# Second rows' DMA transpose placed inside the sequence of loads, with a new load sequence and instruction order

## The chip, the cores and the metric

The kernel runs on one core of a Trainium2 chip. The metric is the device time of one execution in microseconds (us). TensorE (PE in the profile) does matrix products and transposes into PSUM, VectorE (DVE) and ScalarE (ACT) do elementwise work and copy PSUM out, GpSimd (POOL) does small helpers, and SyncE (SP) issues nearly all transfers; ACT's queue issues the rest.

## The reference

Rows of `A_q` (2048 x 512, bf16) are normalized to `xn`. Two branches use them: a gated MLP with 1792 hidden columns, and a short shifted product of `k` and `v` followed by a long causal convolution with a filter as long as the sequence, written with FFTs. The result is `x + s * silu(mlp)`.

```
def reference(A_q, A_k, A_v, A_shift_k, A_ssm_k, A_ssm_D, B_x, B_w_gate, B_w_up, B_w_down):
    def _A_ref(q, k, v, shift_k, ssm_k, ssm_D):
        ks = shift_k.shape[-1]                                  # 4 taps
        k_pad = jnp.pad(k, ((0, 0), (ks - 1, 0), (0, 0)))
        for t in range(ks):
            k_shift = k_shift + k_pad[:, t:t + S, :] * shift_k[:, ks - 1 - t][None, None, :]
        kv = k_shift * v
...
        y = irfft(rfft(kv) * rfft(ssm_k))[:S] + kv * ssm_D
        return q * y
    def _B_ref(x, w_gate, w_up, w_down):
        h = _gelu(x @ w_gate) * (x @ w_up)
        return h @ w_down
    x = A_q
    xn = _layernorm(x, axis=-1)
    s = _A_ref(xn, A_k, A_v, A_shift_k, A_ssm_k, A_ssm_D)
    g = _silu(_B_ref(xn, B_w_gate, B_w_up, B_w_down))
    return x + s * g
```

(The FFT lines are condensed.)

## The kernel before

**Rows.** The 2048 rows lie as 16 tiles of 128, in four groups q = 0 to 3 (first to fourth rows). `ln(q)` normalizes a group: `bn_stats` and `bn_aggr` on DVE, a power on POOL, then `XN`. `xn_transpose(q)` makes `xnT`, the layout that the products need: for q = 0 by PE transposes of `XN`, copied out by ACT and DVE; for q > 0 by one DMA transpose on SP. `xnT` has two buffers, so the third rows take the first rows' one.

**MLP.** `unit(q, m)` is one of 14 column blocks: four matmuls with `Wg`, four with `Wu` (128x512 each; for q = 0 and m < 2 in halves of 256 columns), GELU on ACT into `GE`, and the product `HT` on DVE. `down(q)` multiplies `HT` by `Wd`, 14 matmuls for each row tile.

**Convolution.** It is a two-stage transform written as matmuls. The filter `Hn` (four loads) is transposed by PE into `HTr` (`h_transpose`, 16 transposes a load) and multiplied by the first-stage matrix in `TB` (rows `psall<-HTr,TB`), copied by ACT to `ASH` and stored to the DRAM scratch `ZH`. `kshift(i)` computes the shifted product for a group of rows on DVE into `V` (`KAC`, `KTM` and `V`, eight steps of 128x2048), which needs the loads of `KK`, `V` and the taps `SKR`, spread by POOL to `SKB`. `V` goes through the same stage (rows `psall<-V,TB`) to `ZK`. Second stages read back `BH` and `BK` in 32-row tiles; the filter's spectrum goes to `ZS` and comes back as `HS`. `spectrum(n)` for n = 0 to 7 multiplies (`HB`, `KS` on DVE) and transforms back with `TT`, the DMA transpose of `TB`; results go through `ZI`, come back as `BI`, and a last matmul with `TT` gives y.

**What sets the order.** Nothing is ordered by hand. `Sched.add` records a task with its engine, its estimated duration, what it reads and writes, and a priority; `Sched.run` walks through estimated time, always taking the engine that can start first and on it the task with the lowest priority number among those that could start within `SLACK`. The result fixes the instruction order on each engine; `Trk` adds the semaphore waits. The `P_` numbers are priorities. Loads are tasks of a pseudo-engine `loads`, in the order of the string `ORDER`: a = a single tile of the first rows (odd ones on ACT's queue), h = a quarter of the filter, w = a chunk of `Wg` and `Wu`, k and v = a quarter of `KK` and `V`, x = a later group of rows, d = half of `Wd`, s = `Drow`, `SKR` and the three small pieces of `KK`. All loads are issued ahead of everything else on SP; the DMA transposes, stores and scratch loads come behind the last of them. `hold` puts `N_HOLD` matmuls on zeros between the two halves of the first rows' transposes.

The lines on which the change bears most:

```
order = S.run()
order.sort(key=lambda t: 0 if t is t_zero else 1 if t.eng == "loads" else 2)
for t in order:
    t.emit(t.eng)
```

Of the kernel before, what the change touches and what calls it, by code (L numbers as in the profile page):

```python
# [14 lines left out]
DM = 512  # L15
# [9 lines left out]
ORDER = "a0 a1 h0 a2 a3 w0 h1 w1 h2 w2 h3 s0 w3 k0 v0 w4 x1 k1 v1 d0 d1 k2 v2 k3 v3 x2 x3"  # L25
# [13 lines left out]
P_KB = 30.904
P_PI = -42.641  # L40
P_LN1 = -49.977
P_LN2 = 65.105
P_LN3 = 20.555
N_HOLD = 3
P_H1 = -92.083
P_K1 = 58.537
P_KSH = 8.63
P_KV = -83.839
P_BH = -76.098
P_H2 = -49.07  # L50
P_H2E = 103.626
P_K2 = -54.197
P_MUL = 9.87
P_BO = -5.789
P_ZI = -56.979
P_Q0 = 100.795
P_DN = 126.799
P_GE = -54.936
P_HT = -22.28
P_TA = 11.975  # L60
P_TG = -10.089
P_BI = -97.551
P_Y = -98.812
P_YD = -118.206
P_GX = 100.186
P_OD = -78.816
P_CW = -46.946
P_WS = -85.41
P_SW = -56.976
P_HTR = 9.192  # L70
P_SKB = 105.503
P_SG = 65.13
P_SU = 9.136
# [394 lines left out]
def build_kernel(nc, A_q, A_k, A_v, A_shift_k, A_ssm_k, A_ssm_D, B_w_gate, B_w_up, B_w_down, out):  # L468
    with ExitStack() as es0:
# [414 lines left out]
        def xn_transpose(q):  # L884
            af = gu_tasks[q - 2] if q >= 2 else (skb if q else [])
# [397 lines left out]
```

## Time and profile before

| what | value |
|---|---|
| median of 3 runs | 210.4 us (208.4, 210.4, 211.3) |
| profiled execution | 209.09 us, of which the span is 207.3 us |
| granted TensorE clock, mean | 0.992 |
| DMA traffic | 57.06 MB, mean 275 GB/s |
| ACT copies after the filter's first stage | 16 of 1.0 us |
| store of a filter tile to `ZH`, issue to landing | 6.8 us median |

The profile shows one execution. Its span runs from the first to the last recorded work; the run's own time is 1.8 us longer. "Busy" is the time an engine executes; a wait is put down to whatever came last before the engine went on. The row of busy tenths cuts the span into 40 slices, and DMA traffic by slice shows the loads of the first quarter:

```profile
DMA  6999999999923289999989999997997413397953
GB/s 182 320 365 332 359 394 394 398 418 361 251 68 152 100 274 287 321 307 369 310 272 292 243 304 352 401 353 269 356 298 273 159 54 104 121 343 223 310 219 103
```

One slice is 5.2 us. The DMA engines are full in the first ten slices and nearly idle in the twelfth.

### The profile page before, as it was taken

What the parts mean: (1) busy time and instruction counts of PE and PEld (TensorE: products, weight loads), DVE (VectorE), ACT (ScalarE), POOL (GpSimd) and SP (SyncE); (2) the same over time, 40 slices, a digit from 0 to 9 for tenths busy, and PEclk for the clock granted to TensorE, in tenths of its full rate; (3) what the DMA queues carried; (4) which work ended last, traced back from release to release, by engine and by line L of the source; (5) the groups of instructions that cost most, each with busy time, mean ns of one, the idle gap of its engine ahead of it and who ended that gap; (6) DMA issues with size and microseconds to landing.
All of it is one profiled execution on the core that took longest, in us unless ns stands there. A gap on an engine that the chain in (4) does not pass through costs nothing.

```text
span 207.3 us, 3599 instructions
## 1 busy us (share of the span) xinstructions
PE 191.6 (92%) x1404; PEld 86.3 (42%) x1404; DVE 150.2 (72%) x245; ACT 130.3 (63%) x168; POOL 10.1 (5%) x21
## 2 busy tenths in 40 slices
PE   7699999996199999999998898999999999999993
PEld 2485444442044444343343333334344334444452
DVE  7788289989429989998894384676776672338994
ACT  6245776786066878988966486777787694441111
POOL 2201301003000000000120000000000000000000
PEclk9999999999889999999999999999999999999999
DMA  6999999999923289999989999997997413397953
GB/s 182 320 365 332 359 394 394 398 418 361 251 68 152 100 274 287 321 307 369 310 272 292 243 304 352 401 353 269 356 298 273 159 54 104 121 343 223 310 219 103
DMA packets 43623, 57.06 MB, mean 275 GB/s; under 512 B 11091, under 2 KB 31447, under 8 KB 42582
## 3 DMA queue, kind: packets, MB, share of 16 engines
q1 hardware_dynamic: 36662, 48.18, 70.3%
q10 hardware_dynamic: 6944, 8.65, 12.2%
q8 instruction: 11, 0.18, 0.3%
q14 instruction: 6, 0.05, 0.1%
HBM read 35.78 MB, written 18.87 MB: 264 GB/s over the span
## 4 chain that ended last, share of the span: by engine, by line
PE 65%; DMA 25%; DVE 5%; issue 2%; ACT 2%; SPq 1%; DVEq 0%
PE psall L674 60%; DMA xnT<-XN 13%; DMA HS<-ZS 5%; DMA KK<-in_A_k_dram 5%; PE psall L1022 4%; DMA X<-in_A_q_dram 2%; SPq L650 1%; DVE KS L1087 1%; DVE HB L1087 1%; DVE HT L1129 1%; DVE KTM L1003 1%; ACT xnT L670 1%; PE psall L898 1%; ACT AST L670 0%; PE psall L928 0%
## 5 line engine op out<-in xcount | busy, mean ns | idle before, releaser
L674 PE MATMUL psall<-xnT,Wg 128*128 128x512 bf16 (+1 forms) x232 | 55.3, 376 | 7.5 <-DMA xnT<-XN 6.7
L1129 DVE TENSOR_TENSOR HT<-psall,GE 128x512 bf16<-128x512 f32 x56 | 38.3, 689 | 26.3 <-PE psall L674 23.6
L674 PE MATMUL psall<-xnT,Wu 128*128 128x512 bf16 (+1 forms) x232 | 55.4, 373 | 0.0
L674 PE MATMUL psall<-Wd,HT 128*128 128x512 bf16 (+1 forms) x238 | 51.5, 367 | 0.0
L1126 ACT ACTIVATE GE<-psall 128x512 bf16<-128x512 f32 x56 | 32.3, 600 | 22.9 <-PE psall L674 22.9
L674 PEld LDWEIGHTS psall<-xnT,Wg 128*128 128x128 bf16 x232 | 22.1, 98 | 34.7 <-issue 8.1
L674 PEld LDWEIGHTS psall<-Wd,HT 128*128 128x128 bf16 x238 | 22.9, 98 | 25.7 <-issue 1.3
L674 PEld LDWEIGHTS psall<-xnT,Wu 128*128 128x128 bf16 x232 | 21.6, 98 | 26.6 <-issue 3.7
L670 ACT ACTIVATE BO<-psall 128x1024 bf16<-128x1024 f32 x16 | 16.4, 1025 | 7.1 <-DMA ZI<-BO 3.1
L1155 DVE SCALAR_TENSOR_TENSOR G<-G,psall 128x512 bf16<-128x512 bf16 x12 | 8.2, 687 | 14.6 <-ACT G L1153 14.5
L670 ACT ACTIVATE ASH<-psall 128x1024 bf16<-128x1024 f32 x16 | 15.9, 1023 | 3.9 <-PE psall L674 3.9
L670 ACT ACTIVATE KB<-psall 128x1024 bf16<-128x1024 f32 x16 | 16.0, 1026 | 1.8 <-PE psall L1022 1.4
L1005 DVE TENSOR_TENSOR KAC<-KAC,KTM 128x2048 bf16<-128x2048 bf16 x12 | 15.1, 1262 | 0.2
L1087 DVE TENSOR_TENSOR HB<-KB,HS 128x1024 bf16<-128x1024 bf16 x16 | 11.0, 686 | 5.8 <-DMA HS<-ZS 5.2
L1003 DVE TENSOR_TENSOR KTM<-KK,SKB 128x2048 bf16<-128x2048 bf16 x12 | 14.6, 1217 | 0.1
L1040 ACT ACTIVATE AST<-psall 128x1024 bf16<-128x1024 f32 x11 | 11.1, 1027 | 4.7 <-DMA ZS<-AST 3.0
L863 DVE BATCH_NORM_STATS2 stats<-X 128x6 f32<-128x512 bf16 x16 | 10.5, 675 | 2.0 <-DMA X<-in_A_q_dram 2.0
L1161 ACT ACTIVATE G<-psall 128x512 bf16<-128x512 f32 (+1 forms) x5 | 2.6, 512 | 15.0 <-PE psall L674 15.0
L1087 DVE TENSOR_TENSOR KS<-KB,HS 128x1024 bf16<-128x1024 bf16 x16 | 11.0, 685 | 0.0
L670 ACT ACTIVATE AST<-psall 128x1024 bf16<-128x1024 f32 x9 | 9.2, 1025 | 2.4 <-PE psall L674 2.4
L1153 ACT ACTIVATE G<-psall 128x512 bf16<-128x512 f32 x12 | 7.1, 608 | 5.7 <-PE psall L674 5.5
L674 PE MATMUL psall<-HTr,TB 128*128 128x512 bf16 x32 | 9.5, 395 | 0.4 <-DVE HT L1129 0.4
(73 smaller groups left out, 149.0 us busy)
## 6 DMA issues: line engine op xcount, KB each, us to landing
HS<-ZS SPq DMA_DIRECT2D x16, 512.0 KB, 6.0
ZH<-ASH ACTq DMA_DIRECT2D x16, 256.0 KB, 6.8
BH<-ZH SPq DMA_DIRECT2D x8, 512.0 KB, 5.1
BK<-ZK SPq DMA_DIRECT2D x8, 512.0 KB, 6.1
ZI<-BO ACTq DMA_DIRECT2D x16, 256.0 KB, 3.9
BI<-ZI SPq DMA_DIRECT2D x16, 256.0 KB, 4.4
ZS<-AST SPq DMA_DIRECT2D x11, 256.0 KB, 4.3
ZK<-AST SPq DMA_DIRECT2D x9, 256.0 KB, 3.8
```

Of the source, the lines that this page charges most:

```text
L670: return h.activation(o, i, ACTF.Copy)
L674: return h.matmul(o, lhsT=l, rhs=r, start=st, stop=sp)
L863: t_stats[t] = op([("DVE", 670.0)], lambda e, h, t=t: h.bn_stats(stats[:, t, :], X[:, t, :]), r=[bX[q][t % 4]], w=[bst[t]], rr=[R_X[t]], w ...
L1003: op([("DVE", dur)], lambda e, h, j=j, m=m: h.tensor_tensor(KTM[:, m.slot, :, :], kk(j), sk(j), ALU.mult), r=need + [bSKB[j], a], w=[m], r ...
L1005: op([("DVE", dur)], lambda e, h, m=m: h.tensor_tensor(KAC[:, a.slot, :, :], KAC[:, a.slot, :, :], KTM[:, m.slot, :, :], ALU.add), r=[m], ...
L1022: trk.op("PE", lambda h: h.matmul(ps(s, i)[b, :], lhsT=w(col)[a, :], rhs=data(col)[a, :], start=n < 16, stop=n >= len(todo) - 16, tile_pos ...
L1040: op([("ACT", act(1024))], lambda e, hd, p=p, a=a: hd.activation(ast["K"][a.slot].rearrange("p c d -> p (c d)"), ps(psl(p)), ACTF.Copy, sc ...
L1087: op([("DVE", dve(1024, 2))], lambda e, hd, h=h, k=k, o=o, T=T: hd.tensor_tensor(flat(T, o), flat(KB, kb[h]), flat(HS, hs, (k, 2 * h)), AL ...
L1126: op([("ACT", act(512))], lambda e, h: h.activation(GE[:, g.slot, :], bank(pg), ACTF.Gelu_apprx_tanh), r=[pg], w=[g], rr=lambda: R_bank(pg ...
L1129: op([("DVE", dve(512, 1))], lambda e, h: h.tensor_tensor(HT[:, q % 2, m, :], bank(pu), GE[:, g.slot, :], ALU.mult), r=[pu, g], w=[bHT[q][m]],
L1153: op([("ACT", act(n))], lambda e, h, g=g, pc=pc: h.activation(g, pc(), ACTF.Tanh, scale=0.5), r=[p], w=[bt], rr=lambda p=p: R_bank(p), ww= ...
L1155: op([("DVE", dve(512, 1))], lambda e, h, g=g, pc=pc: h.scalar_tensor_tensor(out=g, in0=g, scalar=1.0, in1=pc(), op0=ALU.add, op1=ALU.mult ...
```

## The change

- The string `ORDER` is new. The four filter loads come right behind the first rows' tiles; weights follow from chunk 4 to chunk 0; and a new entry `t1` puts the second rows' DMA transpose between the loads k2 and v2, so that v2, v1 and x2 are issued behind it on SP.
- For that, `xn_transpose(1)` adds its task to `loads` with the duration `T_XT`, and no longer waits for the tap copies `skb`. The emission loop issues the loads ahead of `t1` first, and from `t1` on those behind it at the place where `t1` stands in the order.
- `hold` and `N_HOLD` go: three matmuls on zeros.
- The transpose of `TB` no longer waits for the last load by name; it follows it on SP anyway.
- The estimate of load times is by a rate for each load instead of by bytes loaded so far, and loads are taken strictly in sequence. `SLACK`, `HEDGE`, `QUEUE`, `DEFER` and all 39 `P_` numbers are new. These set the order alone.

No other instruction is added or removed.

```
-ORDER = "a0 a1 h0 a2 a3 w0 h1 w1 h2 w2 h3 s0 w3 k0 v0 w4 x1 k1 v1 d0 d1 k2 v2 k3 v3 x2 x3"
+ORDER = "a0 a1 h3 a3 h2 a2 h0 h1 k0 w4 w3 x1 s0 w1 v3 k1 w2 w0 x3 d0 k3 d1 v0 k2 t1 v2 v1 x2"
...
+T_XT = 2400.0
...
-P_XT = -23.014
-P_G1 = -95.843
+P_XT = -67.6853007
+P_G1 = -45.5396678
...
-N_HOLD = 3
...
-    SLACK = 90.163
+    SLACK = 96.23327505813286
...
-    QUEUE = {"ACT": 1017.717, "DVE": 26555.1}
+    QUEUE = {"ACT": 1232.4012520764104, "DVE": 429041.2336871297}
...
-    DEFER = 8815.075
+    DEFER = 6968771.228794256
...
-        def hold(e):
-            for i in range(N_HOLD):
...
+        xt_at = {}
         for what in ORDER.split():
             i = int(what[1:])
+            if what[0] == "t":
+                n_load[0] += 1
+                xt_at[i] = n_load[0]
+                continue
...
-            af = gu_tasks[q - 2] if q >= 2 else (skb if q else [])
+            af = gu_tasks[q - 2] if q >= 2 else []
...
-                S.add([("SP", 4400.0)], f, r=bXN[4 * q:4 * q + 4], w=bxnT[q], prio=-1 if q < 3 else P_XT, nbytes=1.6 * 524288, after=af)
+                if q in xt_at:
+                    S.add([("loads", T_XT)], lambda e: f("SP"), r=bXN[4 * q:4 * q + 4], w=bxnT[q], prio=xt_at[q], lat=1500.0)
+                else:
+                    S.add([("SP", 4400.0)], f, r=bXN[4 * q:4 * q + 4], w=bxnT[q], prio=-1 if q < 3 else P_XT, nbytes=1.6 * 524288, after=af)
...
-        g1_tasks = [S.add([("SP", 4400.0)], tt, r=[bF, bTW, bTS], w=[bTT], prio=P_G1, nbytes=1.6 * 589824, after=last_load)]
+        g1_tasks = [S.add([("SP", 4400.0)], tt, r=[bF, bTW, bTS], w=[bTT], prio=P_G1, nbytes=1.6 * 589824)]
...
-        order.sort(key=lambda t: 0 if t is t_zero else 1 if t.eng == "loads" else 2)
+        loads = [t for t in order if t.eng == "loads"]
+        turn = next(i for i, t in enumerate(loads) if not t.nbytes)
+        for t in [t_zero, *loads[:turn]]:
+            t.emit(t.eng)
         for t in order:
-            t.emit(t.eng)
+            for x in loads[turn:] if t is loads[turn] else [t] if t.eng != "loads" and t is not t_zero else []:
+                x.emit(x.eng)
```

**Place 1: the second rows' transpose.** SP's queue from the last loads to the first stores, before:

```order
L650 DMA Wd<-in_B_w_down_dram 128x7x512 x2
L650 DMA KK<-in_A_k_dram 128x2048
L650 DMA V<-in_A_v_dram 128x2048
L650 DMA KK<-in_A_k_dram 128x2048
L650 DMA V<-in_A_v_dram 128x2048
L650 DMA X<-in_A_q_dram 128x2048 x2
L889 DMA_TRANSPOSE xnT<-XN 128x16x128
L1057 DMA_TRANSPOSE TT<-TB 128x18x128
L650 DMA ZK<-AST 128x1024 x3
L650 DMA ZK<-ASX 128x1024
```

and now:

```order
L659 DMA KK<-in_A_k_dram 128x2048
L659 DMA Wd<-in_B_w_down_dram 128x7x512
L659 DMA V<-in_A_v_dram 128x2048
L659 DMA KK<-in_A_k_dram 128x2048
L898 DMA_TRANSPOSE xnT<-XN 128x16x128
L659 DMA V<-in_A_v_dram 128x2048 x2
L659 DMA X<-in_A_q_dram 128x2048
L1066 DMA_TRANSPOSE TT<-TB 128x18x128
L659 DMA ZK<-AST 128x1024 x3
L659 DMA ZK<-ASX 128x1024
```

The transpose `xnT<-XN` moved from behind the last load to ahead of the last three (v2, v1, x2). PE's queue at the end of the first rows and the start of the second rows (the first `Wg` row behind `Wd` is the second rows' first gate matmul), before:

```order
L674 MATMUL psall<-HTr,TB 128x512 x4
L674 MATMUL psall<-xnT,Wu 128x256 x4
L674 MATMUL psall<-HTr,TB 128x512 x4
L674 MATMUL psall<-Wd,HT 128x512 x28
L674 MATMUL psall<-xnT,Wg 128x512 x4
L674 MATMUL psall<-HTr,TB 128x512 x2
L674 MATMUL psall<-xnT,Wu 128x512 x4
```

and now:

```order
L683 MATMUL psall<-Wd,HT 128x512 x4
L683 MATMUL psall<-HTr,TB 128x512 x2
L683 MATMUL psall<-Wd,HT 128x512 x23
L683 MATMUL psall<-V,TB 128x512 x4
L683 MATMUL psall<-Wd,HT 128x512 x5
L683 MATMUL psall<-V,TB 128x512 x2
L683 MATMUL psall<-Wd,HT 128x512 x5
L683 MATMUL psall<-V,TB 128x512 x2
L683 MATMUL psall<-Wd,HT 128x512 x5
L683 MATMUL psall<-xnT,Wg 128x512 x8
```

42 matmuls with `Wd` and 8 with `V` now stand ahead of the second rows, 28 and none before; the last four with `HTr` moved ahead of them too.

**Place 2: the start.** PE's queue behind the warm-up matmuls, before:

```order
L928 MATMUL psall<-ident,Hn 128x128 x16
L898 MATMUL psall<-ident,XN 128x128 x8
L674 MATMUL psall<-AST 128x512 x3
L674 MATMUL psall<-xnT,Wg 128x256 x4
L674 MATMUL psall<-xnT,Wu 128x256 x4
L928 MATMUL psall<-ident,Hn 128x128 x16
L898 MATMUL psall<-ident,XN 128x128 x8
L674 MATMUL psall<-xnT,Wg 128x256 x4
L674 MATMUL psall<-xnT,Wu 128x256 x4
L928 MATMUL psall<-ident,Hn 128x128 x16
L674 MATMUL psall<-xnT,Wg 128x256 x4
L674 MATMUL psall<-xnT,Wu 128x256 x4
```

and now:

```order
L937 MATMUL psall<-ident,Hn 128x128 x32
L910 MATMUL psall<-ident,XN 128x128 x8
L937 MATMUL psall<-ident,Hn 128x128 x32
L910 MATMUL psall<-ident,XN 128x128 x8
L683 MATMUL psall<-HTr,TB 128x512 x4
L683 MATMUL psall<-xnT,Wg 128x512 x8
L683 MATMUL psall<-xnT,Wu 128x512 x4
L683 MATMUL psall<-HTr,TB 128x512 x4
L683 MATMUL psall<-xnT,Wu 128x512 x4
L683 MATMUL psall<-xnT,Wg 128x512 x8
L683 MATMUL psall<-HTr,TB 128x512 x2
L683 MATMUL psall<-xnT,Wu 128x512 x8
```

All filter transposes (`ident,Hn`) and both halves of the first rows' (`ident,XN`) now stand ahead of the first matmul with weights. DVE's queue behind the second-stage matrix's phases, before:

```order
L763 TENSOR_SCALAR TB<-TB 128x1024
L1129 TENSOR_TENSOR HT<-psall,GE 128x512 x2
L671 COPY HTr<-psall 128x8x128
L941 TENSOR_TENSOR HTr<-HTr,Drow 1x512
L1129 TENSOR_TENSOR HT<-psall,GE 128x512 x3
L999 TENSOR_TENSOR KAC<-KK,SKB 128x2048
L1003 TENSOR_TENSOR KTM<-KK,SKB 128x2048
L1129 TENSOR_TENSOR HT<-psall,GE 128x512
L1005 TENSOR_TENSOR KAC<-KAC,KTM 128x2048
L1129 TENSOR_TENSOR HT<-psall,GE 128x512
L863 BN_STATS stats<-X 128x6 x2
```

and now:

```order
L767 TENSOR_SCALAR TB<-TB 128x1024
L1138 TENSOR_TENSOR HT<-psall,GE 128x512
L872 BN_STATS stats<-X 128x6 x2
L873 BN_AGGR mv<-stats 128x2
L872 BN_STATS stats<-X 128x6
L873 BN_AGGR mv<-stats 128x2 x2
L872 BN_STATS stats<-X 128x6
L873 BN_AGGR mv<-stats 128x2
L881 TENSOR_SCALAR mv<-mv 128x4
L1138 TENSOR_TENSOR HT<-psall,GE 128x512 x3
L950 TENSOR_TENSOR HTr<-HTr,Drow 1x512
L1008 TENSOR_TENSOR KAC<-KK,SKB 128x2048
```

The statistics of the second rows (`stats`, `mv`) now stand behind the first product `HT`; before, seven such products and three steps of the shift were ahead of them.

**Place 3: the third rows.** PE's queue from the last filter tile (`BH`) to the second `BK`, before:

```order
L1022 MATMUL psall<-BH,TB 32x512 x16
L674 MATMUL psall<-Wd,HT 128x512 x10
L674 MATMUL psall<-xnT,Wg 128x512 x8
L674 MATMUL psall<-xnT,Wu 128x512 x8
L674 MATMUL psall<-xnT,Wg 128x512 x4
L1022 MATMUL psall<-BK,TB 32x512 x16
L674 MATMUL psall<-xnT,Wu 128x512 x4
L674 MATMUL psall<-xnT,Wg 128x512 x8
L1022 MATMUL psall<-BK,TB 32x512 x16
```

and now:

```order
L1031 MATMUL psall<-BH,TB 32x512 x16
L683 MATMUL psall<-Wd,HT 128x512 x24
L683 MATMUL psall<-xnT,Wg 128x512 x4
L1031 MATMUL psall<-BK,TB 32x512 x16
L683 MATMUL psall<-Wd,HT 128x512 x5
L683 MATMUL psall<-xnT,Wu 128x512 x4
L683 MATMUL psall<-xnT,Wg 128x512 x8
L1031 MATMUL psall<-BK,TB 32x512 x16
```

The first `BK` group moved to four matmuls behind the third rows' first gate matmul, from 20 behind it, and five matmuls with `Wd` moved behind it. On SP the third rows' transpose stands behind two loads of `HS`, and the two loads of `BK` follow it; both were so before, with a `BH` load and stores of `ZS` between.

More of the change, by code (lines that the diff above doesn't have):

```diff
@@ L32 @@
 T_INV = 690.0
+T_XT = 2400.0
 HS_FROM = int(13.29)
-P_ZS = -35.04
-P_HS = 105.448
-P_BK = -29.464
-P_XT = -23.014
-P_G1 = -95.843
[L39 to L43, printed above, removed]
-N_HOLD = 3
[L45 to L73, printed above, removed]
+P_ZS = 91.8946285
+P_HS = 52.5968103
+P_BK = 8.48035155
+P_XT = -67.6853007
+P_G1 = -45.5396678
+P_KB = 3.36553573
+P_PI = -39.790127
+P_LN1 = -111.887859
+P_LN2 = -21.7736545
+P_LN3 = 0.459049962
+P_H1 = -31.771448
+P_K1 = 2.41989469
+P_KSH = -24.6737771
+P_KV = -33.0638954
+P_BH = 31.4158168
+P_H2 = -5.81285766
+P_H2E = 23.8526548
+P_K2 = -87.3940817
+P_MUL = 49.7472247
+P_BO = 57.8816091
+P_ZI = -83.8152
+P_Q0 = -45.3595108
+P_DN = 72.9821729
+P_GE = -15.1315689
+P_HT = -67.0323475
+P_TA = -111.86655
+P_TG = -32.2414312
+P_BI = 61.025623
+P_Y = -32.9204001
+P_YD = -38.4138675
+P_GX = -36.9909855
+P_OD = -26.746681
+P_CW = 24.6371116
+P_WS = 40.2769735
+P_SW = -38.2335702
+P_HTR = 58.126054
+P_SKB = -16.2616284
+P_SG = 57.8491714
+P_SU = 11.9645805
 class Res:
@@ L343, in add @@
         t.n = len(self.tasks)
-        t.opts = [(e, max(d, nbytes / next(bw for most, bw in self.LOAD_BW if self.n_loaded < most)) if e == "loads" else d) for e, d in opts]
-        self.n_loaded += nbytes if opts[0][0] == "loads" else 0
+        t.opts = list(opts)
         t.r, t.w = list(r), list(w)
@@ L387, in run @@
         pipe = 0.0
-        loaded = self.FIRST["loads"] + sum(t.opts[0][1] for t in self.tasks if t.opts[0][0] == "loads")
+        loads = sorted((t for t in self.tasks if t.opts[0][0] == "loads"), key=lambda t: t.prio)
+        loaded = self.FIRST["loads"] + self.LOADED_BY * sum(t.opts[0][1] for t in loads)
+        free["SP"] = loaded - self.SP_LEAD
         ready = [t for t in self.tasks if t.nleft == 0]
@@ L393, in run @@
             for t in ready:
+                if t.opts[0][0] == "loads" and t is not loads[0]:
+                    continue
                 base = 0.0
@@ L432, in run @@
             if eng == "loads":
-                t.end += self.LOAD_LAT
+                loads.pop(0)
+                if st < pipe:
+                    free[eng] = st + (en - st) * self.SHARED_BY
+                t.end = free[eng] + self.LOAD_LAT
             elif t.nbytes:
+                if eng == "SP" and en < loaded:
+                    pipe = max(pipe, loaded)
                 pipe = max(pipe, en + self.DMA_LAT / 2) + t.nbytes / (self.DMA_BW if en > loaded else self.SHARE_BW)
```

40 lines of the change are left out of this document (19 added, 21 removed).

## The prediction

> **What bounds the kernel now.** I read the page's busy shares first, then the list of waits, the chain of work that ended last, and TensorE's timeline where the chain leaves TensorE. From the page, and from the waits of PE:
>
> ```profile
> PE 191.6 (92%) x1404; PEld 86.3 (42%) x1404; DVE 150.2 (72%) x245; ACT 130.3 (63%) x168; POOL 10.1 (5%) x21
> PE psall L674 <- DMA xnT<-XN: 6.7, 2, 5.8
> ```
>
> PE is busy for 92% of the span, and its one long wait, 5.8 us, is for a DMA transpose. So the time is PE's work plus a few holes. The chain shows where the hole lies:
>
> ```profile
> 28.85 8.75 PE psall L674 x42
> 37.60 18.29 DMA xnT<-XN
> 56.03 21.31 PE psall L674 x92
> ```
>
> The second rows' transpose is issued at 37.60 and lands 18.29 us later, at 55.89; only then does PE go on. PE's timeline (start, duration, count):
>
> ```profile
> 9.68 0.61 PE L674 MATMUL psall<-xnT,Wg 128*128 128x256 bf16 x4 [0.50 <-DVE xnT L671]
> ...
> 10.56 1.16 PE L928 MATMUL psall<-ident,Hn 128*128 128x128 bf16 x16
> 11.56 0.61 PE L898 MATMUL psall<-ident,XN 128*128 128x128 bf16 x8
> 12.00 0.60 PE L674 MATMUL psall<-xnT,Wg 128*128 128x256 bf16 x4
> ...
> 28.85 0.61 PE L674 MATMUL psall<-HTr,TB 128*128 128x512 bf16 x2 [0.43 <-DVE HT L1129]
> ...
> 38.36 1.89 PE L674 MATMUL psall<-xnT,Wg 128*128 128x512 bf16 x8
> 40.09 1.89 PE L674 MATMUL psall<-xnT,Wu 128*128 128x512 bf16 x8
> ...
> 43.98 6.21 PE L674 MATMUL psall<-Wd,HT 128*128 128x512 bf16 x28
> 56.03 1.87 PE L674 MATMUL psall<-xnT,Wg 128*128 128x512 bf16 x4 [5.84 <-DMA xnT<-XN]
> 57.69 1.06 PE L674 MATMUL psall<-HTr,TB 128*128 128x512 bf16 x2
> 58.54 1.10 PE L674 MATMUL psall<-xnT,Wu 128*128 128x512 bf16 x4
> 59.48 1.03 PE L674 MATMUL psall<-xnT,Wg 128*128 128x512 bf16 x4
> ```
>
> Eight matmuls take 1.73 us (38.36 to 40.09), so one costs 0.216 us; a group of 16 filter transposes costs 1.0 us and of 8 row transposes 0.44 us (10.56, 11.56, 12.00). From 9.68 PE runs with one gap of 0.43 us until the hole. Behind the hole it is slow: the ten matmuls from 56.03 to 59.48 take 3.45 us instead of 2.16, so the hole costs another 1.3 us. Two stretches worked out by the windows view (PE, PEld, DVE, ACT, POOL busy, granted clock, DMA share, GB/s) agree:
>
> ```profile
> 50.10:60.00 9.90, 4.06 (x14) 1.60 (x14) 4.48 (x5) 1.72 (x3) 0.44 (x1) 0.83 0.85 188
> 60.00:112.80 52.80, 51.74 (x349) 21.59 (x347) 44.99 (x68) 42.56 (x54) 2.39 (x2) 1.00 0.79 260
> 60.00:204.00 144.00, 141.00 (x1115) 60.33 (x1113) 104.74 (x158) 94.99 (x123) 2.39 (x2) 1.00 0.78 257
> ```
>
> The granted clock is 0.83 around the hole and 1.00 behind it. From 60 to 204 PE idles 3.0 us in all.
>
> **Why the transpose is late.** SP's queue by its timeline, and the issues that lie there, with the time to landing as last number:
>
> ```profile
> 35.59 0.43 SPq L650 DMA_DIRECT2D KK<-in_A_k_dram  x1
> ...
> 36.59 0.97 SPq L650 DMA_DIRECT2D X<-in_A_q_dram  x2
> 37.60 15.01 SPq L889 DMA_TRANSPOSE xnT<-XN  x1
> ...
> KK<-in_A_k_dram SPq DMA_DIRECT2D x1, 512.0 KB, 11.6
> X<-in_A_q_dram SPq DMA_DIRECT2D x1, 512.0 KB, 15.7
> ```
>
> The last row load is issued at about 37.1 and lands 15.7 us later, at 52.8; the transpose lands at 55.89, that is 3.1 us behind it. It does not take 18 us, it stands in line. The loads of k3 landed at 35.59 + 11.6 = 47.2, with v3, x2, x3 (1.5 MB) still to come.
>
> **The change, part by part.**
>
> (1) The transpose in the loads. Behind it now stand v2, v1 and x2, again 1.5 MB, so the loads ahead of it carry the bytes that had landed at 47.2. Plus 3.1 us it lands near 50.3. Bounds: not before 47.2, and if it still lands behind everything, 55.9. The three loads behind it come some 3 us later; v1 and x2 feed DVE work of the second and third rows, after 55.
>
> (2) When PE wants it. Ahead of the second rows' first gate matmul PE now has all 32 HTr matmuls (28 before), 112 gate and up, 42 down (28) and 8 V matmuls (none): 194 against 168 of 0.216 us. The 26 more are 5.6 us of work moved into the stretch that was the hole.
>
> (3) The start. All four filter loads stand in front. From the starts and landings of the first filter load and two later transfers:
>
> ```profile
> 1.20 0.42 SPq L650 DMA_DIRECT2D Hn<-in_A_ssm_k_dram  x1
> Hn<-in_A_ssm_k_dram SPq DMA_DIRECT2D x1, 512.0 KB, 4.4
> 4.23 0.60 SPq L650 DMA_DIRECT2D Wu<-in_B_w_up_dram  x1
> Wu<-in_B_w_up_dram SPq DMA_DIRECT2D x1, 256.0 KB, 7.2
> 4.87 1.80 SPq L650 DMA_DIRECT2D Hn<-in_A_ssm_k_dram  x1
> Hn<-in_A_ssm_k_dram SPq DMA_DIRECT2D x1, 512.0 KB, 7.8
> ```
>
> The first landed at 5.6; the third at 12.67, 1.24 us behind the weights ahead of it (11.43). Three more at that pace and one row tile give 9.7; I take 10.1. By 11.43 the old sequence had landed just as many bytes (2.6 MB), which is the upper end. Then 1.0 us of filter transposes, 0.44 us of row transposes and 0.5 us to copy them out (the wait at 9.68): PE's steady work begins at 12.0, between 11.6 and 13.4. Before, it began at 9.68 with three filter groups and one row group (3.44 us) still inside, comparable to 13.1. Gain 1.1 us, between 1.5 and -0.3. The three zero matmuls that go (N_HOLD) stood in this wait, not on the path: 0.
>
> A rule of the Trainium skill, "TensorE: Matmul & The Clock Gate" (What's actually happening), bears on both ends: PE falls to half clock after about 3.4 us idle and needs about 3.4 us of work to come back. By it the slow stretch behind the hole would cost 1.7 us, not the 1.3 of the rows, and the sum would be 0.4 us lower. The trace agrees with the kind (clock 0.83), not with the size. By the same rule the dropped zero matmuls would matter only if the new start idles that long; the gaps I work out there are below 1 us.
>
> (4) DVE now computes the second rows' statistics between the first and the second product HT. From DVE's timeline:
>
> ```profile
> 31.28 1.28 DVE L863 BATCH_NORM_STATS2 stats<-X 128x6 f32<-128x512 bf16 x2 [0.76 <-DMA X<-in_A_q_dram]
> ...
> 34.27 0.17 DVE L872 TENSOR_SCALAR mv<-mv 128x4 f32<-128x4 f32 x1
> ```
>
> That is 3.2 us, starting when x1 lands. That load ends 2.6 MB behind the 11.43 point: five half-megabytes at 1.24 us give 17.6, the mean pace up to 47.2 (10.6 MB in 35.8 us) gives 20.3; I take 18, as only weights and rows lie between. The second HT (0.69 us, row below) then ends at 21.9, and PE, 38 matmuls into its work, wants its bank back at 20.2 unless another is free. I take 1.0 us of wait, between 0 and 4.
>
> (5) Third rows. PE's first BK product now stands four matmuls (0.9 us) behind the third rows' first gate matmuls, 20 before:
>
> ```profile
> 104.50 6.25 SPq L889 DMA_TRANSPOSE xnT<-XN  x1
> 112.38 1.29 SPq L650 DMA_DIRECT2D BK<-ZK  x2
> 112.84 1.89 PE L674 MATMUL psall<-xnT,Wg 128*128 128x512 bf16 x8 [0.87 <-DMA xnT<-XN]
> BK<-ZK SPq DMA_DIRECT2D x8, 512.0 KB, 6.1
> xnT<-XN SPq DMA_TRANSPOSE x3, 8.2
> ```
>
> SP issues BK behind that transpose: 6.3 + 0.5 + 6.1 = 12.9 us after the transpose is issued, whose own landing is 8.2. PE gets to the second rows at 12.0 + 1.0 + 194 x 0.216 = 54.9, and to the third at 112.84 less 6.9 (the terms of the sum below that lie ahead) and less 1.1 (five down matmuls that now come later), 104.8. The transpose can be issued near 94 (the last second-row HT, then some 5 us of statistics and normalizing), so it lands in time, and BK near 107 against a want at 105.7. I take 0.8 us, between 0 and 4.
>
> (6) All else (new P_ numbers, SLACK, QUEUE, DEFER) sets an order I cannot price from the trace. The 3.0 us of idle between 60 and 204 stay, and I add 0.7 us since ACT, 42.56 of 52.8 us busy from 60 to 112.8, gets the same work in some 5 us less; between -1.5 and +2.5.
>
> **The sum**, against the profiled execution (span 207.3, run 209.1): hole -5.8, slow clock behind it -1.3, gap at 28.85 -0.4, start -1.1, statistics +1.0, BK +0.8, middle +0.7: -6.1, which gives 203.0. That execution was 1.3 us below the median of 210.4; against the median it is 204.3. I forecast 203.7, between the two.
>
> **Rivals.**
>
> - *DVE becomes the bound.* Two groups of the page price its queue:
>
> ```profile
> L1129 DVE TENSOR_TENSOR HT<-psall,GE 128x512 bf16<-128x512 f32 x56 | 38.3, 689 | 26.3 <-PE psall L674 23.6
> L1005 DVE TENSOR_TENSOR KAC<-KAC,KTM 128x2048 bf16<-128x2048 bf16 x12 | 15.1, 1262 | 0.2
> ```
>
> Ahead of the first V matmuls DVE has 14 products HT (9.6 us), the statistics (3.2) and 14 steps of the shift (17.7): 30.5 us, from 15.5 on, when PE has the first sums. It ends at 46 with no wait at all, and PE, 171 matmuls in, wants the result at 49.9, less an ACT copy. For it: x1, the shift taps and v0 can each hold DVE up there. Against it: 23.6 us of HT's old idle time were waits for PE, not for DVE's own queue. With 6 us of DVE waits PE loses 3: 206.7.
> - *The second hole moves to the third rows.* If SP issues their transpose at 104.5 as before (it stands behind two loads of HS that wait for stores), it lands at 112.7, PE waits 7.9 us there, 7.0 more than the 0.87 of before, and all is given back: 210. It costs nothing if issued by 96.6, and a microsecond for each one later.
> - *Slower.* The same place, one step further: with BK 12.9 us behind a transpose issued at 104.5 PE's queue stands until 117.4, 11.7 us in all, which is 10 more than the sum holds, and a wait of that length brings the slow clock, 1.3 us: 214.3. From an issue near 99.5 on the change is worth nothing by it. Against it: the last second-row products come 7 us earlier than before.
> - *It does not do what it says*: the transpose still lands behind all loads, at 55.9. PE wants it at 54.9, since it has 26 matmuls more to do first: 204.7 all the same.
>
> **How the numbers follow.** Chances: forecast 0.62, DVE bound 0.14, given back 0.13, slower 0.06, late transpose 0.05. A measurement of this kernel can tell about 2% (4.2 us) from no change. The forecast case (200.5 to 206) counts as faster but for a tenth of it, the late transpose mostly so, a part of the DVE case too: faster 0.63. Given back, the rest of the DVE case and that tenth: 0.31. Slower 0.06. The range runs from 200.5, where the uncertain costs take their low ends, to 208.5, which takes in the DVE case and a part of given back.
>
> **What would show it.** In the profile after: no wait of PE for xnT near 50 to 56, and the clock 1.00 there; the transpose landing between 48 and 53 while three loads still run; the first gate matmuls near 13 and those of the second rows near 55; waits of PE below 2 us near 20 and 104. I am wrong if PE waits over 3 us for the third rows' transpose or BK, if DVE runs without a gap from 17 to 58 and PE waits for V, or if the start comes after 14.

## The result and the profile after

| | before | after |
|---|---|---|
| median of the runs | 210.85 us (208.40 to 211.51) | 202.29 us (201.79 to 204.92, 4 runs) |
| profiled execution | 209.09 us, span 207.3 | 201.79 us, span 200.0 |
| mean granted TensorE clock | 0.992 | 1.00 |

The ratio is 0.961, 95% interval 0.950 to 0.971: faster by 2.9 to 5.0%. Two later sets of runs of the same kernel gave 203.21 and 202.98 us beside 210.82 and 211.18 for the kernel before. The ratios leave out executions over 1.5% slower than the fastest of the same kernel, the medians do not.

The busy shares on the page of the changed kernel, then its list of waits of PE (us in total, times, longest):

```profile
PE 189.7 (95%) x1389; PEld 86.5 (43%) x1401; DVE 150.4 (75%) x245; ACT 130.1 (65%) x168; POOL 8.6 (4%) x21
```

```profile
PE psall L1031 <- ACT BO L679: 1.4, 1, 1.4
PE psall L683 <- DVE AST L722: 1.2, 1, 1.2
PE psall L683 <- DVE HTr L680: 1.1, 1, 1.1
PE psall L683 <- ACT BO L679: 1.0, 1, 1.0
PE psall L1031 <- DMA BK<-ZK: 0.9, 1, 0.9
```

PE's work is the same within the records that a trace loses, its share rose from 92 to 95%, and no wait for `xnT` is left in the list; the longest wait is 1.4 us. PE's timeline of the changed kernel (start, duration, count, idle time ahead) at the places of the prediction:

```profile
13.51 0.81 PE L683 MATMUL psall<-HTr,TB 128*128 128x512 bf16 x3 [1.05 <-DVE HTr L680]
...
54.25 1.24 PE L683 MATMUL psall<-Wd,HT 128*128 128x512 bf16 x5
55.33 1.89 PE L683 MATMUL psall<-xnT,Wg 128*128 128x512 bf16 x8
...
103.00 1.04 PE L683 MATMUL psall<-xnT,Wg 128*128 128x512 bf16 x4
104.94 0.44 PE L1031 MATMUL psall<-BK,TB 32*32 32x512 bf16 x16 [0.91 <-DMA BK<-ZK]
...
126.73 0.44 PE L1031 MATMUL psall<-BK,TB 32*32 32x512 bf16 x16 [1.44 <-ACT BO L679]
128.20 1.90 PE L683 MATMUL psall<-xnT,Wu 128*128 128x512 bf16 x8 [1.03 <-ACT BO L679]
```

The second rows begin at 55.33, right behind the five `Wd` matmuls and at full speed (eight in 1.73 us). In the kernel before they began at 56.03 with 26 fewer matmuls done, 5.6 us of work, and then ran 1.3 us slow: the same work would have been done at 62.9. So 7.6 us were won up to that place, more than the 7.3 by which the span fell. At the third rows, with the five `Wd` matmuls that now come later, 112.84 - 1.08 = 111.76 stands against 103.00: 8.8 us. Behind them 1.5 is lost again up to PE's last matmul, which ends at 196.7 instead of 204.0; from there to the end it is 3.3 us in both.

SP's queue and the time from issue to landing (last number) of the second rows' transpose, both of the changed kernel:

```profile
37.68 1.77 SPq L659 DMA_DIRECT2D KK<-in_A_k_dram  x1
39.49 10.42 SPq L898 DMA_TRANSPOSE xnT<-XN  x1
49.96 1.06 SPq L659 DMA_DIRECT2D V<-in_A_v_dram  x2
```

```profile
xnT<-XN SPq DMA_TRANSPOSE x1, 13.8
```

It lands at 39.49 + 13.8 = 53.3, 2.0 us ahead of the want, while v2, v1 and x2 are still under way: the issue of the transpose holds SP's queue for 10.42 us, so v2 is issued only at 49.96.

### The profile page after: what moved, and what is told of

It reads as the page before. It is cut to its first block, busy times and chain, and to the rows that moved or that the text cites. A ratio compares the mean times of both kernels' runs of the same rounds, so it can differ in the third digit from the quotient of the medians.

```text
span 200.0 us, 3581 instructions
## 1 busy us (share of the span) xinstructions
PE 189.7 (95%) x1389; PEld 86.5 (43%) x1401; DVE 150.4 (75%) x245; ACT 130.1 (65%) x168; POOL 8.6 (4%) x21
## 4 chain that ended last, share of the span: by engine, by line
PE 67%; DMA 13%; DVE 7%; issue 5%; ACT 4%; SPq 1%; POOLq 1%; POOL 1%; ACTq 0%
PE psall L683 63%; DMA ZI<-BO 5%; PE psall L1031 4%; DMA Hn<-in_A_ssm_k_dram 3%; DMA BH<-ZH 3%; DMA BK<-ZK 3%; ACT BO L679 2%; DVE KTM L1012 1%; DVE HT L1138 1%; DVE HTr L680 1%; DVE XN L885 1%; DVE stats L872 1%; ACT G L1162 1%; SPq L659 1%; DVE KAC L1014 1%
## 5 line engine op out<-in xcount | busy, mean ns | idle before, releaser
L683 PE MATMUL psall<-xnT,Wu 128*128 128x512 bf16 (+1 forms) x232 | 55.2, 373 | 1.0 <-ACT BO L679 1.0
L683 PE MATMUL psall<-xnT,Wg 128*128 128x512 bf16 (+1 forms) x232 | 53.8, 372 | 0.0
L683 PE MATMUL psall<-Wd,HT 128*128 128x512 bf16 (+1 forms) x232 | 50.6, 367 | 0.3 <-issue 0.2
L1164 DVE SCALAR_TENSOR_TENSOR G<-G,psall 128x512 bf16<-128x512 bf16 x12 | 8.1, 685 | 12.7 <-ACT G L1162 12.7
L1012 DVE TENSOR_TENSOR KTM<-KK,SKB 128x2048 bf16<-128x2048 bf16 x12 | 15.2, 1264 | 0.1
L1014 DVE TENSOR_TENSOR KAC<-KAC,KTM 128x2048 bf16<-128x2048 bf16 x12 | 14.6, 1220 | 0.2
L683 PE MATMUL psall<-HTr,TB 128*128 128x512 bf16 x29 | 7.7, 380 | 1.2 <-DVE HTr L680 1.1
```

The source lines that it names most:

```text
L683: return h.matmul(o, lhsT=l, rhs=r, start=st, stop=sp)
L1012: op([("DVE", dur)], lambda e, h, j=j, m=m: h.tensor_tensor(KTM[:, m.slot, :, :], kk(j), sk(j), ALU.mult), r=need + [bSKB[j], a], w=[m], r ...
L1014: op([("DVE", dur)], lambda e, h, m=m: h.tensor_tensor(KAC[:, a.slot, :, :], KAC[:, a.slot, :, :], KTM[:, m.slot, :, :], ALU.add), r=[m], ...
L1164: op([("DVE", dve(512, 1))], lambda e, h, g=g, pc=pc: h.scalar_tensor_tensor(out=g, in0=g, scalar=1.0, in1=pc(), op0=ALU.add, op1=ALU.mult ...
```

## The experiments

The prediction gave the hole of 5.8 us to two things together: the transpose lands earlier (the place on SP), and PE asks for it later (26 more matmuls ahead). My theory A was that the place is what counts; the rival, that the sequence and the order of the instructions do it. The hole is the landing less the moment at which PE asks, so the table below has these two for both kernels and for runs 1 to 4 and 6 to 8; the times of the runs follow one by one.

| kernel | transpose issued, lands | PE asks | hole | median us |
|---|---|---|---|---|
| before | 37.60, 55.9 | 50.2 | 5.84 | 210.85 |
| before, early place | 36.58, 54.5 | 49.9 | 4.68 | 210.72 |
| before, early place, loads behind `TT` | 36.09, 56.2 | 49.8 | 6.57 | 211.85 |
| before, early place, four stores later | 36.61, 50.2 | 50.0 | 0.38 | 205.96 |
| after, transpose last | 41.79, 58.9 | 56.2 | 2.75 | 206.37 |
| new loads, old numbers | 38.79, 54.6 | 54.7 | 0 | 207.21 |
| old loads with t1, new numbers | 38.45, 53.3 | 53.5 | 0 | 207.66 |
| after | 39.49, 53.3 | 55.3 | 0 | 202.29 |
| after, four stores later | 39.80, 50.3 | 55.3 | 0 | 204.85 |

("Asks" is the end of PE's last work ahead of the hole. The runs were made in sets, each with the kernel before beside it: it had 210.82 us beside runs 1, 2, 5 and 11, 211.46 beside runs 3, 4, 6 and 7, and 211.18 beside runs 8 to 10.)

**1. The place undone.** The changed kernel, with the transpose issued behind v2, v1 and x2; the order on every other engine stays.

```
-            for x in loads[turn:] if t is loads[turn] else [t] ...
+            for x in loads[turn + 1:] + loads[turn:turn + 1] if t is loads[turn] else [t] ...
```

> The changed kernel with one thing undone: on SP the second rows' transpose stands behind v2, v1 and x2 again; every other engine's order is unchanged. Theory A (its place in the line of loads carries the gain): it lands some 2.4 us behind the last load, near 58 to 60, PE waits 2.5 to 5 us for it at 55.3 and may start again at the slow clock, 205 to 209 us. Theory B (the 26 matmuls moved ahead of the second rows cover it wherever it stands): PE waits under 1 us, 202 to 203.5 us.

Measured: 206.37 us (204.44 to 208.20), ratio 0.982 (0.975 to 0.990). PE's timeline, and the issues of the last load and the transpose with their times to landing:

```profile
58.99 1.90 PE L683 MATMUL psall<-xnT,Wg 128*128 128x512 bf16 x8 [2.75 <-DMA xnT<-XN]
```

```profile
X<-in_A_q_dram SPq DMA_DIRECT2D x1, 512.0 KB, 13.4
xnT<-XN SPq DMA_TRANSPOSE x1, 17.1
```

A hole is back, 2.75 us, as theory A had it. The last load is issued at 40.87 and lands at 54.3, the transpose at 41.79 + 17.1 = 58.9, 4.6 us behind it. So about half of the gain is there without the place, and the place is worth the other half, some 3 to 4 us of the medians, in this order.

**2. The place alone.** The kernel before, with the transpose issued ahead of v3, x2 and x3; nothing else moves.

```
+        late = [t for t in order if t.eng == "loads"][-3:]
         for t in order:
-            t.emit(t.eng)
+            if t not in late:
+                t.emit(t.eng)
+            for x in late if t is t_xt[1] else []:
+                x.emit(x.eng)
```

> The old kernel with one thing changed: on SP the second rows' transpose stands ahead of its last three loads (v3, x2, x3); every other engine's order and the load sequence are the old ones. Theory A: the hole at 50.1 closes, PE waits under 1 us, and with the slow clock gone the gain is 6.5 to 7.1 us, 203 to 204 us. Theory A with both halves needed (place and work): the transpose lands at 52 to 54 as in the changed kernel, PE waits 2 to 4 us since it has nothing else to do, 205.5 to 208 us. Theory B (order and sequence carry the gain): under 1.5 us gained, 208.5 us or more.

Measured: 210.72 us (209.40 to 214.87), ratio 1.001 (0.997 to 1.006): nothing. PE's timeline, the time to landing, and the windows (PE, PEld, DVE, ACT, POOL busy, granted clock, DMA share, GB/s):

```profile
54.61 1.86 PE L674 MATMUL psall<-xnT,Wg 128*128 128x512 bf16 x4 [4.68 <-DMA xnT<-XN]
56.27 1.06 PE L674 MATMUL psall<-HTr,TB 128*128 128x512 bf16 x2
57.12 1.91 PE L674 MATMUL psall<-xnT,Wu 128*128 128x512 bf16 x4
58.83 1.59 PE L674 MATMUL psall<-xnT,Wg 128*128 128x512 bf16 x4
60.26 0.59 PE L674 MATMUL psall<-HTr,TB 128*128 128x512 bf16 x2
60.69 1.03 PE L674 MATMUL psall<-xnT,Wu 128*128 128x512 bf16 x4
```

```profile
xnT<-XN SPq DMA_TRANSPOSE x1, 17.9
```

```profile
48.00:50.00 2.00, 1.93 (x9) 0.69 (x7) 2.00 (x3) 1.91 (x3) 1.51 (x1) 1.00 1.29 117
50.00:52.00 2.00, 0.00 (x0) 0.00 (x0) 2.00 (x3) 0.00 (x0) 0.28 (x1) 1.00 1.11 212
...
58.00:60.00 2.00, 2.00 (x6) 0.74 (x5) 0.69 (x1) 0.39 (x1) 0.00 (x0) 0.51 1.14 257
```

The transpose is issued ahead of three loads and still lands at 54.5, only 1.4 us earlier than before. And those 1.4 us are eaten behind the hole: the 16 matmuls from 54.61 take 6.08 us until 60.69 instead of 3.46, 2.6 us lost at a clock of 0.5 in this trace, where the kernel before lost 1.3. Theory A in its simple form has fallen; the time is the one theory B named, though run 4 gives another reason for it. Between 48 and 52 the DMA engines are busy but move only 117 and 212 GB/s. What the transpose shares them with is the question of the next two runs.

**3. Are the three loads what it shares the engines with?** As 2, with v3, x2 and x3 issued only behind the transpose of `TB`.

```
-            for x in late if t is t_xt[1] else []:
+            for x in late if t is g1_tasks[0] else []:
```

> As the old order with the early transpose, but v3, x2 and x3 are issued behind the transpose of TB too, so no load stands right behind the second rows' transpose. Theory L (the loads behind it took its share of the DMA engines): it lands by 51.5 instead of 54.5, PE waits under 1.7 us, 205 to 207.5 us. Theory Z (the four filter stores issued from 44 to 46 did): still near 54, 209.5 to 211.5 us. Theory X (the transpose alone holds the engines for 7 us, whatever stands beside it): still near 54.

Measured: 211.85 us (209.75 to 215.14), ratio 0.998 (0.994 to 1.002): nothing again. The time to landing in the trace, which is of an execution of 213.25 us:

```profile
xnT<-XN SPq DMA_TRANSPOSE x1, 20.1
```

It lands at 36.09 + 20.1 = 56.2, no earlier than in 2. The loads that follow the transpose on SP are not what holds it, and theory L has fallen.

**4. Or the filter stores?** As 2, with four stores of the filter's first stage (`ZH<-ASH`, 256 KB each, on ACT's queue at 43.94 to 46.12 us) issued behind the first GELU of the second rows.

```
+        zh = sorted(zh_tasks, key=order.index)[10:14]
+        order = [t for t in order if t not in zh]
+        at_ge = order.index(t_ge[1, 0]) + 1
+        order[at_ge:at_ge] = zh
```

> As the old order with the early transpose, but the four filter stores that ACT issued from 44 to 46 are issued behind its first GELU of the second rows. Theory Z: the transpose lands by 51.5, PE waits under 1.7 us, 205 to 207.5 us. Theories L and X: it still lands near 54, and the time is that of the early transpose in the old order, 210 to 211.5 us.

Measured: 205.96 us (204.06 to 207.32), ratio 0.970 (0.962 to 0.978). PE's timeline and the time to landing:

```profile
50.34 1.02 PE L674 MATMUL psall<-xnT,Wg 128*128 128x512 bf16 x4 [0.38 <-DMA xnT<-XN]
```

```profile
xnT<-XN SPq DMA_TRANSPOSE x1, 13.6
```

Issued at the same time as in 2 (36.61), it lands at 50.2, 4.3 us earlier, and the hole is gone, with the slow stretch behind it. This is theory Z: 1 MB of stores on another engine's queue stood beside the transpose and put it off; theory X, that it takes as long whatever stands beside it, has fallen. The traces show the sharing. By their bytes, `q1` is SP's queue and `q10` ACT's. The rows give packets, MB and share of the DMA engines, first of run 2 from 50 to 54, then of this run from 48 to 50, where ACT's queue has no row:

```profile
q10 hardware_dynamic: 472, 0.87, 73.0%
q1 hardware_dynamic: 482, 0.38, 35.6%
```

```profile
q1 hardware_dynamic: 1270, 0.49, 102.8%
```

The early place and the later stores together are worth 5.5 us in the old order (211.46 less 205.96). Some is lost again: PE waits 1.49 us at 55.0 for an `ASH` copy by ACT, whose queue issues the four stores first, until 53.8. The later stores with the transpose in its old place were not tried.

**5. The warm-up matmuls.** The kernel before, without the three matmuls on zeros of `hold`.

```
-            for i in range(N_HOLD):
+            for i in range(0):
```

> The old kernel without the three matmuls on zeros, all else in place. Theory: they stood in a wait and cost nothing, the time is the old one within 0.5 us. Rival (they kept the clock up): the clock falls at the start and the time is 1.3 us longer.

Measured: 211.12 us, ratio 1.001 (0.998 to 1.004). The 1.3 us of the rival would be a ratio of 1.006, outside the interval: no use of them is seen in the old start. The wait ahead of the first gate matmul grows from 0.50 to 1.15 us instead, and that matmul starts at 9.77, not 9.68.

**6. Half of the change: the new loads.** The changed kernel with the old `P_` numbers, `SLACK`, `HEDGE`, `QUEUE` and `DEFER`.

> The changed kernel with the old priorities and the old SLACK, HEDGE, QUEUE and DEFER; load sequence, t1 and the estimate of loads are the new ones, so the order is found by the new scheduler with the old numbers. Ahead of the second rows' first gate matmul PE has 28 matmuls with Wd, 8 with V and all with HTr. Theory S (the load sequence with t1 makes the room, the numbers only polish): 202 to 205.5 us. Rival N (the new numbers carry the gain): 207 us or more.

Measured: 207.21 us (206.68 to 212.12), ratio 0.978 (0.971 to 0.984). That is about 4 us of gain, half of the whole, and at the border of what rival N named; the new loads alone do not make theory S's 202 to 205.5.

**7. The other half: the new numbers.** The changed kernel with its numbers, but the old `ORDER` with `t1` in it.

```
-ORDER = "a0 a1 h3 a3 h2 a2 h0 h1 k0 w4 w3 x1 s0 w1 v3 k1 w2 w0 x3 d0 k3 d1 v0 k2 t1 v2 v1 x2"
+ORDER = "a0 a1 h0 a2 a3 w0 h1 w1 h2 w2 h3 s0 w3 k0 v0 w4 x1 k1 v1 d0 d1 k2 v2 k3 t1 v3 x2 x3"
```

> The changed kernel with the old load sequence, and t1 put ahead of its last three loads (v3, x2, x3); the new numbers stay. Ahead of the second rows' first gate matmul PE has 37 matmuls with Wd, 4 with V and all with HTr, so most of the moved work. Theory W (work moved ahead plus the early place are what counts, not the load sequence): 201.5 to 204.5 us. Rival S (the new sequence is needed): 206 us or more.

Measured: 207.66 us (207.17 to 208.54), ratio 0.982 (0.977 to 0.987). Rival S named this. Both halves are without the hole (table) and gain about 4 us each, and yet are 4 to 5 us behind the whole. Most of the loss is at the other end of the program. The chain of work that ended last in this run, where it leaves PE, its last row, and PE's last row:

```profile
172.52 15.02 PE psall L683 x73
187.54 0.02 issue
187.57 1.24 DVE G L1221
...
203.22 0.29 DVE G L1173
```

```profile
196.93 1.14 PE L683 MATMUL psall<-BI,TT 128*128 128x512 bf16 x4 [0.83 <-DMA BI<-ZI]
```

From 187.57 on DVE alone sets the end: its closing products and sums are 16 us of work, and it begins them at 187.57, where the whole change begins them at 179.62 (row below), as PE begins its first `BI` group at 186.50 here and at 178.32 there. PE is done at 198.1 and the span ends at 206.0, 7.9 us later instead of 3.3; the half with the new loads has a tail of 6.8 us and PE waits 2.4 us for `BI` besides. DVE as the bound is thus real, though at a place that the prediction did not look at. DVE's timeline of the changed kernel:

```profile
179.62 1.22 DVE L1221 SCALAR_TENSOR_TENSOR G<-psall,G 128x1024 bf16<-128x1024 f32 x1
```

**8. The same stores in the changed kernel.** Its last four filter stores, issued behind the first GELU of the second rows (the edit of 4, with the slice 12 to 16).

> The changed kernel with its last four filter stores (4 x 256 KB, in the profiled run issued on ACT's queue at 41.01, 43.42, 44.52 and 49.78 us) issued behind the first GELU of the second rows. Theory Z (the filter stores on ACT's queue share the DMA engines with the second rows' transpose and put off its landing): the transpose, which landed at 53.3 us, lands 2 to 4 us earlier, at 49.5 to 51.5, as it did by 4.3 us when the same was done to the old order. Rival P (the place on SP's queue alone sets the landing): it lands at 52.5 to 53.5 as before. Both expect no gain in time, because PE asks for these rows at 55.3 us only, behind 5 us of other work: 201 to 204 us, or up to 2 us more, where the first load of the filter's spectra, which needs all the stores, is issued later than its 60.2 us. A time of 199 us or less would show that I have the end of the wait wrong.

Measured: 204.85 us (203.29 to 205.57), ratio 0.971 (0.964 to 0.978), beside 0.963 (0.959 to 0.967) for the unaltered kernel in the same set of runs. The time to landing:

```profile
xnT<-XN SPq DMA_TRANSPOSE x1, 10.5
```

It lands at 50.3, against 53.1 in the run of the unaltered kernel beside it (issued at 39.66, landing after 13.4 us): 2.8 us earlier. Theory Z holds here too. Time is not won, as both theories said, because PE asks at 55.3. Whether the 1.9 us that it is behind are real is left open by the intervals, which overlap. Its profile shows 1.4 us more span: the first `BH`, which needs the stores, is asked for at 63.08 instead of 60.15 and the third rows begin 1.7 us later, and behind 128.95 sixteen matmuls take 5.2 us instead of 3.6, at a clock that fell to 0.50.

**9. What the changed kernel still loses.** Its waits at 126.7 and 128.2 us go back to ACT, which had no free `BO` buffer: the store issued at 115.69 took 9.9 us to land, while SP issued four loads of `HS` (512 KB each, 114.43 to 117.94). Four buffers instead of two, the other two over `AST` buffers that are done by then; the order stays.

```
+        BO4 = [BO[:, 0, :, :], BO[:, 1, :, :], AST[:, 1, :, :], AST[:, 2, :, :]]
+        R_BO4 = [*R_BO, *R_AST["K"][1:3]]
...
-copy(e, hd, flat(BO, bo[h]), ps(psl(pi[h]))),
+copy(e, hd, BO4[(2 * n + h) % 4].rearrange("p c d -> p (c d)"), ps(psl(pi[h]))),
```

> The changed kernel with four BO buffers instead of two: the third and fourth are laid over two AST buffers whose last stores are issued at 113.2 us; the order of the instructions stays. In the profile of the changed kernel PE waits 1.4 and 1.0 us at 126.7 and 128.2 us for ACT, which itself waited 3.9 us for the store of BO of 115.7 us to land (9.9 us). Theory B (these waits are the price of the two buffers and lie on the path to the end): both waits go, and the span is 1.5 to 2.4 us shorter, 198 to 200.5 us of time. Rival Q (the DMA engines are the bound there, 1 MB of the HS loads queues ahead: whoever is asked next waits as long): the waits move to HB or KB behind the late HS and BK loads at 118 to 132 us, and the time stays within 0.7 us of the changed kernel's.

> The changed kernel unaltered, as the yardstick of the three runs beside it on the same chip: 201 to 204 us.

Measured: 199.86 us (198.92 to 200.96), ratio 0.948 (0.943 to 0.953); the unaltered kernel beside it 202.98, ratio 0.963 (0.959 to 0.967). The intervals do not touch: this version beats both kernels, the changed one by 3.1 us of the medians. PE's row and ACT's row for the third buffer in this run, and one stretch of the windows of the changed kernel and of this one:

```profile
125.11 0.41 PE L1031 MATMUL psall<-BK,TB 32*32 32x512 bf16 x8 [0.16 <-DVE HT L1140]
```

```profile
121.16 1.02 ACT L679 ACTIVATE AST<-psall 128x1024 bf16<-128x1024 f32 x1
```

```profile
105.00:170.00 65.00, 62.46 (x630) 25.54 (x631) 39.60 (x62) 47.16 (x61) 0.00 (x0) 1.00 0.78 258
```

```profile
105.00:170.00 65.00, 64.84 (x628) 26.59 (x626) 40.86 (x64) 48.44 (x63) 0.00 (x0) 1.00 0.80 262
```

ACT copies at 121.16 instead of 125.65, PE waits 0.16 us there instead of 1.44, and its idle time from 105 to 170 falls from 2.5 to 0.2 us. The waits did not move elsewhere in this stretch, so theory B holds.

**10. And the wait for `BK`.** As 9, with PE's first group on `BK` behind the five `Wd` matmuls that followed it.

```
+        pes = [t for t in order if t.eng == "PE"]
+        nxt = pes[pes.index(t_k2[0]) + 1]
+        order.remove(t_k2[0])
+        order.insert(order.index(nxt) + 1, t_k2[0])
```

> As the run with four BO buffers, and PE's first group that reads BK put behind the five down projection matmuls that follow it (5 x 0.216 us). In the profile of the changed kernel PE waited 0.9 us for BK at 104.9 us. If that wait is a matter of order alone, it falls to 0 and the span is another 0.9 us shorter, 197 to 200 us of time. If what comes next waits for KB instead (ACT's copies behind the group run 105.5 to 108.1 us and begin 1.1 us later), the gain is 0.3 us or nothing.

Measured: 199.68 us (197.90 to 201.11), ratio 0.945 (0.940 to 0.950). The wait of 0.9 us for `BK` is gone from PE's list, but the time is not told apart from that of 9: the intervals overlap, and the medians differ by 0.2 us.

**11. The yardstick** of runs 1, 2 and 5: the changed kernel again.

> The changed kernel itself, as the yardstick on the same chip: 201.5 to 203 us.

Measured: 203.21 us (201.00 to 204.57), ratio 0.956 (0.948 to 0.965); the second rows begin at 54.77, the transpose lands at 52.6.

## Why the prediction was right, and where it was not

The forecast of 203.7 us lies 1.4 us from the median, and the sum for the profiled execution said 203.0 where 201.8 was measured. The mechanism held: no wait for `xnT`, clock 1.00, the second rows near 55. Two of its terms were wrong and cancelled by chance, and the landing was 3 us off without effect.

- *Hole and slow clock, -7.1, and the gap, -0.4.* With the start and the statistics the forecast up to the second rows was -7.6, and 7.6 us were won. The 194 matmuls take 41.8 us from 13.51 to 55.33, so PE lost nothing on the way; for the end of the gap the sum gave no reason, and it came true all the same.
- *(1) Landing near 50.3.* It landed at 53.3. The step that failed is the 47.2 for the loads ahead: k2, the last of them, is issued 2.1 us later than k3 was and takes 13.2 us instead of 11.6, so it lands at 50.9. The 3.1 us behind it were 2.4. That term is no constant: it was 2.8 in run 4 (k3 landed at 47.4), but 7.4 in run 2 (k3 at 47.1), where only the four stores differ, and 4.6 in run 1. The prediction priced only SP's queue; the stores on ACT's queue, whose absence moved the landing by 4.3 us (run 4) and 2.8 us (run 8), were in the trace and had no term. The margin of 2.0 us at 55.33 covered the error. The three loads behind it came 5 to 6 us later than before and not some 3 (v2 landed at 55.2, x2 at 57.8; before, v3 at 49.1 and x3 at 52.8), since SP's queue is held while it issues the transpose; no wait of PE came of it.
- *(2) PE asks at 54.9.* It asked at 55.33 (54.77 and 55.31 in the repeats). This part, counted out of the order, was the sure one, and run 1 shows that it alone brings about half.
- *(3) Start, -1.1.* Steady work began at 13.5 (12.7 and 12.8 in the repeats) and not at 12.0; against the 13.1 of the kernel before that is about nothing. The failed step is "0.5 us to copy them out" and the loads as the only limit: PE's transposes ended at 12.4, not 11.5, and then it waited 1.05 us for `HTr`. DVE's timeline of the changed kernel shows why:

```profile
10.57 0.68 DVE L680 COPY HTr<-psall 128x1024 bf16<-128x1024 bf16 x1
11.17 0.73 DVE L885 TENSOR_SCALAR XN<-X,mv 128x512 bf16<-128x512 bf16 x2
11.81 1.41 DVE L680 COPY HTr<-psall 128x1024 bf16<-128x1024 bf16 x2
13.14 0.41 DVE L680 COPY xnT<-psall 128x512 bf16<-128x512 bf16 x1
...
18.17 1.29 DVE L872 BATCH_NORM_STATS2 stats<-X 128x6 f32<-128x512 bf16 x2 [0.37 <-DMA X<-in_A_q_dram]
...
21.66 1.88 DVE L1138 TENSOR_TENSOR HT<-psall,GE 128x512 bf16<-128x512 f32 x3
```

  With all four filter loads in front, the copies of all filter quarters fall together, and DVE works without a gap from 10.2 to 13.5.
- *(4) Statistics, +1.0.* They cost nothing. The times were right (x1 landed for 18.17, forecast 18; the second HT at 21.7 to 22.3, forecast 21.9), but PE did not wait; that it had another bank free is inferred. This and the start nearly cancelled, by luck.
- *(5) BK, +0.8.* Measured 0.91. The third rows were asked for at 103.0 (forecast 104.8), their transpose issued at 92.97 (forecast near 94).
- *(6) Middle, +0.7.* Between the second and the third rows 1.2 us more were won, and 1.5, `BK` included, lost behind: the rest of the program costs 0.3, where +1.5 was forecast with `BK`. Run 9 names the largest piece of the loss, the two `BO` buffers.
- *Rivals.* DVE as the bound did not come about in the first rows; it did at the end in run 7. Given back at the third rows and the slower case needed an issue past 96.6 and 99.5: it was 92.97. The case that the transpose is still last was priced at 204.7, with a landing at 55.9; run 1 gave 58.9 and 206.4.
- *The clock.* An idle time of 2.75 us (run 1) left it at 1.00; 4.68 (run 2), 5.84 (before) and 6.25 us (run 5) did not. The price behind them was 2.6, 1.3 and 1.8 us, so in these three traces it does not grow with the idle time. The Trainium skill's rule of about 3.4 us idle, "TensorE: Matmul & The Clock Gate" (What's actually happening), agrees with which of them slowed, and 1.7 us, an estimate by its figures, lies among the prices. One row does not fit: in run 8 the clock fell to 0.50 (130 to 132 us) behind two waits of 1.35 and 1.03 us, while the changed kernel's two waits of 1.44 and 1.03 us at the same place left it at 1.00.

What the prediction did not say, and the runs show: the place, which names the change, is worth nothing in the old order with the stores beside it, 5.5 us there together with later stores, and 3 to 4 us in the new order.

## What to carry to other kernels

A wait for a transfer is its landing less the moment of asking: work out both for every variant, since a change may move either. The landing depends on what all queues give the DMA engines at that time, not on the place in its own queue alone, so list the stores of the other engines beside a transfer before moving it. Half of a new order can win a wait and lose part of it elsewhere: both halves here closed the hole and gave up 4 to 5 us of the whole gain, most of it at the end, so read the tail of each variant before judging it.

## What the hardware showed that I had not expected

While the second rows' DMA transpose is under way, the DMA engines are busy and move little. The windows of run 1, where the transpose lands at 58.9 and the last load at 54.3:

```profile
50.00:52.00 2.00, 2.00 (x11) 0.82 (x10) 2.00 (x3) 0.74 (x2) 0.00 (x0) 1.00 1.30 403
52.00:54.00 2.00, 2.00 (x11) 0.94 (x10) 2.00 (x3) 2.00 (x3) 0.00 (x0) 1.00 1.15 100
54.00:56.00 2.00, 2.00 (x11) 0.80 (x9) 1.97 (x2) 1.51 (x2) 0.00 (x0) 1.00 1.28 170
56.00:58.00 2.00, 0.24 (x2) 0.00 (x0) 1.97 (x3) 0.22 (x1) 0.00 (x0) 1.00 1.16 179
```

From 403 GB/s the rate falls to 100 to 179, with a DMA share above 1 throughout. Of the 417 packets from 52 to 54, 392 are under 512 bytes, all on SP's queue; ACT's queue moves nothing then, and 0.20 MB from 56 to 58. (The transpose of `TB`, issued at 54.02, is in these rows too.) In the changed kernel the same stretch is 48 to 52 (103 and 229 GB/s at shares of 0.77 and 1.13, between 327 and 379). That each transpose also puts off what is beside it, and k2 among it, fits these rates, but no run tried it alone.
